# Windowed attention feeding a gated MLP on one core: loads and a shift issued at other steps, block 1's two products mixed, three small copies moved

## The chip, the cores and the metric

The kernel runs on one core of a Trainium2 chip. The metric is the device time of one execution in microseconds. The kernel before took 322.61 us as the median of 3 runs, which lay between 320.56 and 323.91 us.

A core has a tensor engine (PE in the profile, with its weight loads as PEld), a vector engine (DVE), a scalar engine (ACT) and GpSimd (POOL). Each runs its own list of instructions in order and waits on semaphores for the others. SP is a queue that issues transfers and computes nothing. GpSimd issues transfers too, as instructions in its list: while one is being issued, or is waiting, what stands behind it on GpSimd waits as well. The same holds on SP.

## The reference, cut to what matters

```python
# q, k, v: (8 batches, 8 heads, 576 positions, 64 dims), float32
scores = q @ k.T / 8, masked to 0 <= pos_q - pos_k < 64
attn   = softmax(scores)
x      = attn @ v                     # then (4608 tokens, 512 = heads x dims)
h      = x @ w_in                     # (4608, 2048)
g      = h * clip(h + 3, 0, 6) / 6
out    = g @ w_out                    # (4608, 512)
```

Each query sees only the 64 latest keys, so attention is cheap and the two products with w_in and w_out make most of the work.

## The kernel before, in words

**Attention.** A batch has 8 heads, worked on as 4 pairs. The code counts pairs t = 0 to 31, with b = t // 4 the batch and g = t % 4 the pair in it. Pairs 0 to 3 have code of their own (`t_k`, `t_q`, `s_early`, `pv_early`, `x_early`). Every later pair goes through the same steps. `turn` (line 274) transposes its keys and queries on the tensor engine, `turned` (281) copies them out, keys on DVE and queries on ACT. `s_first` and `s_rest` (294, 308) make the scores. `weights` (314 to 333) takes exponentials on ACT and multiplies them by 0/1 band masks, from pair 8 on GpSimd: one product P (326), then one product Pz for each of the two heads (329). `pv` (402) multiplies the masked weights by the values, `pv_out` (411 to 426) divides by the row sums on DVE, and `x_` (440) puts the result, transposed by a transfer of SP's, into xT, the MLP's input. Pairs 4 to 7 use `x_turned` (455 to 461) instead, a transpose on the tensor engine and a copy on ACT.

**Values.** `load_v` (138) brings a batch's values into a tile Un in two large transfers (parts 0 and 1), and 32 rows of a second tile Us in a small one (part 2). `shift` (158, 159) fills the rest of Us with two SP transfers from Un, moved by 32 rows. `pv` needs both: from its third matmul on it reads Us. Tiles alternate between even and odd batches. For batch 0 the shifted tile is made by seven DVE or GpSimd copies instead (`shift_early`, 151 and 153).

**MLP.** Tokens go in 9 blocks of 512. The first product of a block has 16 units, one for each 128 columns of w_in (line 485, 4 matmuls each), each followed by one activation on ACT (497) and one product on DVE (498) into gT. The second product has 4 groups of 128 tokens, each of 4 units (521, 4 matmuls of gT with w_out), and after the last unit a copy on ACT (527) and a transfer out on SP (529). Units stand in a queue `moe`. `weave(n)` emits the next n. `queue_block(kb)` appends a block: it starts with two units left over from the block before, spreads the others that are left over between the 16 first units, and then adds half of the block's own second units.

**Order.** From pair 7 on the loop is `group(t, n)`: `pv(t)`, `turn(t+2)`, scores and weights of pair t+1, `pv_out(t)`, `x_(t)`, and n units of the MLP. Group 7 takes 4 units and groups 8 to 11 also take 4 each: the 12 first units of block 1 that are left, then its 8 queued second units. From group 12 on a group takes 6 units. Behind a group's own instructions come the loads for the next batch. For batch 3 these are: parts 0 and 1 of the values behind group 7; keys and queries of pair 0 and then part 2 of the values behind group 8; keys and queries of pairs 1 to 3 behind groups 9 to 11; and the shift behind group 9. For batches 4 to 7: keys and queries whole behind the first group of the batch before, values behind its second group, the shift behind its third.

**Pairs 4 to 7 and batch 2.** While these pairs go through the loop at line 810, GpSimd issues batch 2's loads. One-element copies into `seen` (lines 778, 808, 835) make GpSimd wait until a given tile is ready, and so hold the loads back. The shift of batch 2 (line 825) stands behind the four outputs of block 0 on SP.

Of the kernel before, what the change touches and what calls it, by code (L numbers as in the profile page):

```python
# [31 lines left out]
VO = 8  # L32
# [4 lines left out]
def kernel(  # L37
# [9 lines left out]
    nc = tc.nc  # L47
    B, H, S, _ = q.shape
    DM, FF = moe_w_in.shape
    NT = B * S  # L50
    NG = H // 2
    SP = S // R
    NW = S // W
    NM = (S + P - 1) // P
    NFC = FF // P
# [27 lines left out]
    xT = consts.tile([P, NG, XR], BF16, name="xT")  # L83
# [31 lines left out]
    def load_qk(b, n=NG, first=0):  # L115
        t = staged[b] if first else stage.tile([P, H, RL * D], BF16, name="qk9", tag="qk")
        hs = slice(2 * first, 2 * (first + n))
        for z, src in enumerate((k, q)):
            nc.gpsimd.dma_start(
                out=t[halves[z], hs], in_=src[b, hs].rearrange("h (p r) d -> p h (r d)", r=RL)  # L120
            )
        return t
# [8 lines left out]
    def load_v(b, whole=False, part=slice(None)):  # L131
        loads = (
            (0, Un[b % 2][:, 0], 2 * P), (2 * P, Un[b % 2][:, 1], 2 * P),
            *(((W, Us[b % 2][:, 0], 2 * P), (W + 2 * P, Us[b % 2][:, 1], 2 * P)) if whole
              else ((4 * P, Us[b % 2][3 * P // 4 : P, 1], W),)),
        )
        for m, to, n in loads[part]:
            nc.gpsimd.dma_start(  # L138
                out=to[:, :, VO : VO + P],
                in_=v[b, :, m : m + n, :].rearrange("h (p r) d -> p h (r d)", r=2),  # L140
            )

    def pads(b, memset):
        for t in (Un[b % 2], Us[b % 2]):
            memset(t[:, :, :, 0:VO], 1.0)
            memset(t[:, :, :, VO + P : VW], 1.0)
# [8 lines left out]
    def shift(b):  # L155

        un, us = Un[b % 2], Us[b % 2]
        nc.sync.dma_start(out=us[0 : P - 32], in_=un[32:P])
        nc.sync.dma_start(out=us[P - 32 : P, 0], in_=un[0:32, 1])
# [60 lines left out]
    def t_q(t):  # L220
        b, g = divmod(t, NG)
        tp = transposed_heads(ps_h, staged[b][0], g)
        nc.scalar.copy(
            out=QT[t][:].rearrange("q (p r) -> q p r", r=R), in_=tp[:].rearrange("q r p -> q p r"),
        )
        for h in range(2):
            nc.vector.tensor_copy(out=QZ[t][halves[h], h], in_=QT[t][halves[h], S - W : S])

    def t_k(t):
        b, g = divmod(t, NG)  # L230
        tp = transposed_heads(ps_acc, staged[b][1], g)
        nc.vector.tensor_copy(
            out=KT[t % 4][:, W:].rearrange("q (p r) -> q p r", r=R),
            in_=tp[:].rearrange("q r p -> q p r"),
        )

    def s_early(t):

        kt, qt = KT[t], QT[t]
        sc = [ps_t.tile([P, NM - 1, 2, W], F32, name="sc", tag="bk") for _ in range(2)]  # L240
        sl = ps_t.tile([P, 2, W], F32, name="sl", tag="bk")

        def off(to, n):
            nc.tensor.matmul(
                to, lhsT=ident[:], rhs=outside[:].unsqueeze(1).to_broadcast([P, n, W]), start=True, stop=False
            )

        for h in range(2):
            off(sc[h][:].rearrange("p m a w -> p (m a) w"), NW - 1)
        for w in range(NW - 1):  # L250
            for h in range(2):
                nc.tensor.matmul(
                    sc[h][:, w // 2, w % 2], lhsT=kt[halves[h], w * W : w * W + P],
                    rhs=qt[halves[h], w * W : (w + 1) * W], start=False, stop=w == NW - 2,
                )
        off(sl[:], 2)
        nc.tensor.matmul(sl[:], lhsT=kt[:, S - W : S + W], rhs=QZ[t][:], start=False, stop=True)
        for h in range(2):
            nc.scalar.activation(
                out=Pz[t][:, h].rearrange("p m a w -> p (m a w)"),  # L260
                in_=sc[h][:].rearrange("p m a w -> p (m a w)"), func=EXP, scale=scale,
            )
        nc.scalar.activation(out=Pl[t][:, :, 0:W], in_=sl[:], func=EXP, scale=scale)
# [187 lines left out]
    def x_turned(t):  # L451
        b, g = divmod(t, NG)
        opg, opg0 = opgs.pop(t)
        tp = ps_t.tile([P, S], BF16, name="xp", tag="bk")
        nc.tensor.transpose(out=tp[:, 0:W], in_=opg0[:].rearrange("p h d -> p (h d)"), identity=ident[0:D, 0:D])
        for m in range(NM - 1):
            nc.tensor.transpose(
                out=tp[:, W + m * P : W + (m + 1) * P],
                in_=opg[:, m // 2, m % 2].rearrange("p h d -> p (h d)"), identity=ident[:],
            )  # L460
        nc.scalar.copy(out=xT[:, g, b * S : b * S + S], in_=tp[:])
# [72 lines left out]
    moe = deque()  # L534

    left = []

    def queue_block(kb, kept=2 * NG):

        f = first_units(kb)  # L540
        moe.extend(left[:2])
        del left[:2]
        n = len(left)
        for i, unit in enumerate(f):
            moe.extend(left[i * n // NFC : (i + 1) * n // NFC])
            moe.append(unit)
        left[:] = second_units(kb)
        n = len(left) - kept
        moe.extend(left[:n])
        del left[:n]  # L550
# [10 lines left out]
    def complete(kb, fcs, pair=()):  # L561
        unit, hidden = units[kb]
        for fc in fcs:
            unit(fc, (NG - 1,), act=fc not in pair)
            if fc in pair[1:]:
                for x in pair:
                    hidden(x)
        for _ in fcs:
            moe.popleft()

    def weave(n):
        for _ in range(min(n, len(moe))):
            moe.popleft()()
# [131 lines left out]
    warm(ps_h, 4, W)  # L705
    t_k(0)
    t_q(0)
    t_k(1)
    t_q(1)
    s_early(0)  # L710
    t_k(2)
    t_q(2)
    s_early(1)
    t_k(3)
    t_q(3)
    s_early(2)
    for m in range(1, NM):
        shift_early(m, nc.vector.tensor_copy)
    s_early(3)
    warm(ps_acc, 4)  # L720
# [23 lines left out]
    def group(t, n):  # L744

        if t >= 2 * NG:
            pv(t)
        if t + 2 < T:
            turn(t + 2)
        if t + 1 < T:  # L750
            host = t + 2
            if host >= T:
                hosts[host] = [ps_h.tile([P, 8 * P], BF16, name=name, tag="bk") for name in ("tk", "tq")]
            s = s_first(t + 1, host)
            weights(t + 1, s, s_rest(t + 1))
        if t >= 2 * NG:
            pv_out(t)
        if t + 2 < T:
            turned(t + 2, 0)
        if t >= 2 * NG:  # L760
            x_(t)
        weave(2)
        if t + 2 < T:
            turned(t + 2, 1)
        weave(n - 2)
# [10 lines left out]
    def behind(t):  # L776

        nc.gpsimd.tensor_copy(out=seen[:], in_=opgs[t][1][0:1, 0, 0:1])
# [16 lines left out]
    for t in range(n, n + 4):  # L795
        if t < n + 3:
            turn(t + 1)
        s = s_first(t, min(t + 1, n + 3))

        def copies():  # L800
            if t < n + 3:
                turned(t + 1, 0)
                turned(t + 1, 1)

        weights(t, s, s_rest(t), own, copies)
        if t < n + 3:
            weave((4, 2, 2)[t - n])
    nc.gpsimd.tensor_copy(out=seen[:], in_=P0[(n + 3) % 4][0:1, 0, 0, 0:1])
    staged[2] = load_qk(2, 1)
    for t in range(n, n + 4):  # L810
        pv(t, t % 2 == 0)
        pv_out(t)
        behind(t)
        if t < n + 2:
            load_v(2, part=(slice(0, 1), slice(1, 3))[t - n])
        else:
            load_qk(2, 1, t - n - 1)
        if t > n:
            x_turned(t - 1)
        if t < n + 3:  # L820
            weave(1)
    turn_two(2 * NG)
    weave(len(moe))
    late[0] = 1
    shift(2)
    queue_block(1)
    u, some = units[1][0], range(NG - 1)
    u(0, some, ps_t)
# [2 lines left out]
    x_turned(n + 3)  # L831
    u(3, some, to=pair_bank()[0])
    complete(1, range(4))
    pads(3, nc.gpsimd.memset)
    nc.gpsimd.tensor_copy(out=seen[:], in_=xT[0:1, NG - 1, S : S + 1])
    load_qk(2, 1, 3)
    group(2 * NG - 1, 4)
    load_v(3, part=slice(0, 2))
    for t in range(2 * NG, T):
        b, g = divmod(t, NG)  # L840
        if g == 0 and b > 2:
            queue_block(b - 1)
        group(t, -(-len(moe) // (NG - g)))
        if t == 2 * NG:
            staged[3] = load_qk(3, 1)
            load_v(3, part=slice(2, 3))
        elif b == 2:
            load_qk(3, 1, g)
        if g == 0 and 3 <= b < B - 1:
            staged[b + 1] = load_qk(b + 1)  # L850
        if g == 1 and 3 <= b < B - 1:
            load_v(b + 1)
        if g == 1 + (b > 2) and b + 1 < B:
            shift(b + 1)
    late[0] = 2
    queue_last(NTB - 2)
    flag = flagged()
# [35 lines left out]
```

## Time and profile before

| | before |
|---|---|
| median of 3 runs | 322.61 us (320.56 to 323.91) |
| the profiled execution | 321.83 us |
| its span, first to last instruction | 320.0 us |
| granted TensorE clock, mean | 0.996 |
| PE busy | 302.5 us (95%) |
| DVE busy | 181.1 us (57%) |
| ACT busy | 184.3 us (58%) |
| POOL busy | 124.1 us (39%) |

A row of the timeline gives the start, the duration, the engine, the line of the kernel, the operation, what it writes and reads, how many instructions are merged in it, and in brackets how long its engine was idle before it and what ended that. A row of the waits gives who waited for whom, the total, the number of times and the longest. A row of the transfers gives the queue, the number, the size of each, and the median time from issue to landing. "issue" as a releaser means that the profile shows nothing that the engine waited for.

### The profile page before, as it was taken

How to read it: one execution, taken by the hardware profiler on the slowest of the kernel's cores; microseconds unless marked ns; L12 is line 12 of the kernel's file. 1: busy time of each engine (PE TensorE's matmuls, PEld its weight loads, DVE VectorE, ACT ScalarE, POOL GpSimd, SP SyncE). 2: the span in 40 equal slices, each digit the busy share in tenths (PEclk: the TensorE clock that was granted, in tenths of full speed). 3: DMA queues.
4: the chain of work that ended last, by engine and by line, in shares of the span. 5: the costliest groups of instructions: out<-in, count | busy, mean ns of one | idle time of the engine just before them, and what ended most of it. 6: DMA issues, size and time to landing. Idle time of an engine off the chain costs nothing.

```text
span 320.0 us, 10694 instructions
## 1 busy us (share of the span) xinstructions
PE 302.5 (95%) x4566; PEld 152.2 (48%) x4608; DVE 181.1 (57%) x415; ACT 184.3 (58%) x345; POOL 124.1 (39%) x169
## 2 busy tenths in 40 slices
PE   7889998889999999999999999999999999999992
PEld 3454454444545555555555555555544444444440
DVE  5776747588747753775377627762776156334200
ACT  2737665578657764776477547764773366454310
POOL 8971204669785435553446335633330000000000
PEclk9999999999999999999999999999999999999998
DMA  7999995989999932994299339934021200100021
GB/s 93 164 203 207 207 189 116 173 146 111 179 124 167 131 116 88 167 128 117 88 155 140 108 98 154 144 102 103 5 63 43 84 33 0 69 33 34 36 74 66
DMA packets 57592, 35.67 MB, mean 111 GB/s; under 512 B 39872, under 2 KB 51648, under 8 KB 57536
## 3 DMA queue, kind: packets, MB, share of 16 engines
q0 software_dynamic: 35904, 18.81, 45.9%
q1 hardware_dynamic: 21632, 16.08, 20.6%
q8 instruction: 38, 0.62, 0.8%
q14 instruction: 18, 0.15, 0.1%
HBM read 37.62 MB, written 9.44 MB: 147 GB/s over the span
## 4 chain that ended last, share of the span: by engine, by line
PE 86%; DMA 5%; DVE 2%; issue 2%; ACT 2%; POOL 1%; SPq 0%; POOLq 0%; ACTq 0%
PE hT L485 37%; PE acc L521 35%; PE o L402 3%; PE s L308 3%; PE acco L521 2%; DMA V<-V 2%; PE tk L274 2%; DMA qk<-in_k_dram 2%; DMA xT<-opl 1%; POOL qk L108 1%; PE tq L274 1%; PE hTo L485 1%; DVE opl L426 0%; DVE V L151 0%; PE xp L373 0%
## 5 line engine op out<-in xcount | busy, mean ns | idle before, releaser
L498 DVE SCALAR_TENSOR_TENSOR gT<-t,hT 128x512 bf16<-128x512 bf16 x141 | 95.7, 686 | 77.7 <-ACT t L497 76.9
L485 PE MATMUL hT<-xT,win 128*128 128x512 bf16 x552 | 132.1, 379 | 0.9 <-ACT xT L376 0.3
L521 PE MATMUL acc<-wout,gT 128*128 128x512 bf16 x518 | 126.1, 379 | 2.4 <-issue 1.3
L497 ACT ACTIVATE t<-hT,half_const 128x512 bf16<-128x512 f32 x141 | 95.7, 689 | 50.0 <-PE hT L485 48.1
L485 PEld LDWEIGHTS <-win 128*128 128x128 bf16 x576 | 55.6, 98 | 66.2 <-issue 1.0
L521 PEld LDWEIGHTS <-gT 128*128 128x128 bf16 x576 | 54.3, 98 | 62.8
L329 POOL TENSOR_TENSOR Pz<-e,band 128x512 bf16<-128x512 bf16 x48 | 54.2, 1146 | 0.5 <-ACT e L321 0.4
L326 POOL TENSOR_TENSOR P<-e,first 64x256 bf16<-64x256 bf16 x24 | 15.9, 661 | 84.7 <-ACT e L317 84.6
L527 ACT COPY osb<-acc 128x512 f32<-128x512 f32 x34 | 19.9, 586 | 43.7 <-PE acc L521 43.7
L321 ACT ACTIVATE e<-s 128x512 bf16<-128x512 f32 x56 | 30.2, 593 | 0.9 <-PE s L308 0.7
L281 DVE COPY KT<-tk 128x576 bf16<-128x576 bf16 x28 | 21.0, 749 | 5.3 <-ACT e L317 4.5
L138 POOL DMA_DIRECT2D V<-in_v_dram x22 | 17.9, 819 | 11.6 <-DMA win<-in_moe_w_in_dram 5.2
L426 DVE TENSOR_TENSOR opl<-o,recs 128x256 bf16<-128x256 f32 x52 | 19.6, 419 | 0.5
L281 ACT COPY QT<-tq 128x576 bf16<-128x576 bf16 x28 | 17.8, 637 | 1.5 <-PE tq L274 1.5
L411 DVE TENSOR_REDUCE sums<-o 128x10 f32<-128x20 f32 x26 | 4.5, 175 | 24.3 <-PE o L402 24.3
L402 PEld LDWEIGHTS <-Pz 64*64 64x64 bf16 x1008 | 11.6, 108 | 13.3 <-issue 11.5
L308 PE MATMUL s<-QT,KT 64*64 64x64 bf16 x896 | 14.7, 195 | 0.5 <-issue 0.5
L317 ACT ACTIVATE e<-tk 64x128 bf16<-64x128 f32 x28 | 7.6, 270 | 12.5 <-PE tq L294 12.5
L402 PE MATMUL o<-V,Pz 64*64 64x65 bf16 x936 | 13.6, 195 | 1.2 <-DMA V<-V 1.2
L274 PE MATMUL tk<-ident,qk 64*64 64x64 bf16 x504 | 13.9, 195 | 0.3 <-DMA qk<-in_k_dram 0.3
L274 PE MATMUL tq<-ident,qk 64*64 64x64 bf16 x504 | 13.7, 195 | 0.4 <-DMA qk<-in_q_dram 0.4
L274 PEld LDWEIGHTS <-qk 64*64 64x64 bf16 x1008 | 11.5, 106 | 3.1 <-issue 1.7
(102 smaller groups left out, 196.6 us busy)
## 6 DMA issues: line engine op xcount, KB each, us to landing
out_dram<-osb SPq DMA_DIRECT2D x36, 256.0 KB, 2.3
V<-in_v_dram POOLq DMA_DIRECT2D x16, 256.0 KB, 5.7
V<-V SPq DMA_DIRECT2D x6, 432.0 KB, 4.3
qk<-in_k_dram POOLq DMA_DIRECT2D x4, 576.0 KB, 6.7
qk<-in_q_dram POOLq DMA_DIRECT2D x4, 576.0 KB, 9.7
wout<-in_moe_w_out_dram POOLq DMA_DIRECT2D x2, 1024.0 KB, 18.8
qk<-in_q_dram POOLq DMA_DIRECT2D x12, 144.0 KB, 4.3
qk<-in_k_dram POOLq DMA_DIRECT2D x12, 144.0 KB, 3.8
```

Of the source, the lines that this page charges most:

```text
L274: nc.tensor.transpose(out=hosts[t][z][halves[h], r * W : (r + 1) * W], in_=staged[b][halves[z], 2 * g + h, r * D : (r + 1) * D], identity= ...
L281: (nc.scalar.copy if z else nc.vector.tensor_copy)(out=(QT[t % 4][:] if z else KT[t % 4][:, W:]).rearrange("q (p r) -> q p r", r=RL), in_= ...
L308: nc.tensor.matmul(ss[h][halves[i], c, m, r], lhsT=keys(t, h, W * (w - 1), r), rhs=QT[t % 4][halves[h], w * W : (w + 1) * W], start=True, ...
L321: nc.scalar.activation(out=e[:].rearrange("p c m r w -> p (c m r w)"), in_=ss[h][:].rearrange("p c m r w -> p (c m r w)"), func=EXP, scale ...
L329: muls[h].tensor_tensor(out=Pw[t % 4][:, h].rearrange("p c m r w -> p (c m) (r w)"), in0=e[:].rearrange("p c m r w -> p (c m) (r w)"), in1 ...
L402: nc.tensor.matmul(o[i][halves[c], c0 : c0 + D + 1], lhsT=p, rhs=vt[:, hh, v0 : v0 + D + 1], start=(r == 0), stop=(r == 1), skip_group_che ...
L426: nc.vector.tensor_tensor(out=opg[:, :, i], in0=ov[i][:, 0:4, 1 : D + 1].rearrange("p (m h) d -> p m h d", h=2), in1=rec[:, i, 0:4].rearra ...
L485: nc.tensor.matmul(hT, lhsT=win16[:, g, fc * P : (fc + 1) * P], rhs=xT[:, g, t0 : t0 + TB], start=(g == 0), stop=(g == NG - 1),)
L497: nc.scalar.activation(out=t1[:], in_=hT, func=RELU, bias=half_const[:], scale=1.0 / 6.0)
L498: nc.vector.scalar_tensor_tensor(out=gT[:, fc, :], in0=t1[:], scalar=1.0, in1=hT, op0=MIN, op1=MULT)
L521: nc.tensor.matmul(acc, lhsT=gT[:, fc, ts * P : (ts + 1) * P], rhs=wout16[:, fc, :], start=(fc == 0), stop=(fc == NFC - 1),)
L527: nc.scalar.copy(out=osb[:], in_=acc)
```

## The change

Five things change.

1. The query copies QZ of pair 3 (line 227) move on DVE from ahead of the shifted values to between the copies for m = 2 and m = 3.
2. Batch 2: part 0 of the values is issued ahead of the keys and queries of pair 0, behind a new one-element copy from batch 1's last value tile. Parts 1 and 2 follow behind pair 4, keys and queries of pairs 1 and 2 behind pairs 5 and 6 (before: 6 and 7), those of pair 3 behind group 7 (before: ahead of it). The shift is issued at pair 6, ahead of the last output of block 0. Two one-element copies go.
3. Block 1's queued units are put in a new order: f stands for a first unit, z for a second one. Groups 7 to 11 emit f f f z | f f f z | f f f f | f f z z | z z z z in place of twelve f and eight z.
4. Batch 3: pair 0 and part 0 of the values behind group 8, pair 1 and then parts 1 and 2 behind group 9, pairs 2 and 3 behind groups 10 and 11, the shift behind group 10. Block 2 is queued with four leftover units in front, where it had two.
5. Batches 4 to 7: keys and queries come pair by pair behind the four groups of the batch before, in place of one load of the whole. Values and shift stay at their groups.

```diff
@@ -223,6 +223,8 @@
         nc.scalar.copy(
             out=QT[t][:].rearrange("q (p r) -> q p r", r=R), in_=tp[:].rearrange("q r p -> q p r"),
         )
+
+    def padded(t):
         for h in range(2):
             nc.vector.tensor_copy(out=QZ[t][halves[h], h], in_=QT[t][halves[h], S - W : S])
 
@@ -535,11 +537,11 @@
 
     left = []
 
-    def queue_block(kb, kept=2 * NG):
+    def queue_block(kb, kept=2 * NG, lead=2):
 
         f = first_units(kb)
-        moe.extend(left[:2])
-        del left[:2]
+        moe.extend(left[:lead])
+        del left[:lead]
         n = len(left)
         for i, unit in enumerate(f):
             moe.extend(left[i * n // NFC : (i + 1) * n // NFC])
@@ -705,16 +707,22 @@
     warm(ps_h, 4, W)
     t_k(0)
     t_q(0)
+    padded(0)
     t_k(1)
     t_q(1)
+    padded(1)
     s_early(0)
     t_k(2)
     t_q(2)
+    padded(2)
     s_early(1)
     t_k(3)
     t_q(3)
     s_early(2)
-    for m in range(1, NM):
+    for m in (1, 2):
+        shift_early(m, nc.vector.tensor_copy)
+    padded(3)
+    for m in range(3, NM):
         shift_early(m, nc.vector.tensor_copy)
     s_early(3)
     warm(ps_acc, 4)
@@ -805,24 +813,28 @@
         weights(t, s, s_rest(t), own, copies)
         if t < n + 3:
             weave((4, 2, 2)[t - n])
+    nc.gpsimd.tensor_copy(out=seen[:], in_=Us[1][0:1, 1, 0, VO : VO + 1])
+    load_v(2, part=slice(0, 1))
     nc.gpsimd.tensor_copy(out=seen[:], in_=P0[(n + 3) % 4][0:1, 0, 0, 0:1])
     staged[2] = load_qk(2, 1)
     for t in range(n, n + 4):
         pv(t, t % 2 == 0)
         pv_out(t)
-        behind(t)
-        if t < n + 2:
-            load_v(2, part=(slice(0, 1), slice(1, 3))[t - n])
-        else:
-            load_qk(2, 1, t - n - 1)
+        if t < n + 3:
+            behind(t)
+        if t == n:
+            load_v(2, part=slice(1, 3))
+        elif t < n + 3:
+            load_qk(2, 1, t - n)
         if t > n:
             x_turned(t - 1)
+        if t == n + 2:
+            shift(2)
         if t < n + 3:
             weave(1)
     turn_two(2 * NG)
     weave(len(moe))
     late[0] = 1
-    shift(2)
     queue_block(1)
     u, some = units[1][0], range(NG - 1)
     u(0, some, ps_t)
@@ -831,27 +843,28 @@
     x_turned(n + 3)
     u(3, some, to=pair_bank()[0])
     complete(1, range(4))
+    f, z = [moe.popleft() for _ in range(NFC - 4)], list(moe)
+    moe.clear()
+    moe.extend(f[0:3] + z[0:1] + f[3:6] + z[1:2] + f[6:] + [z[2], z[4], z[3]] + z[5:])
     pads(3, nc.gpsimd.memset)
-    nc.gpsimd.tensor_copy(out=seen[:], in_=xT[0:1, NG - 1, S : S + 1])
+    group(2 * NG - 1, 4)
     load_qk(2, 1, 3)
-    group(2 * NG - 1, 4)
-    load_v(3, part=slice(0, 2))
     for t in range(2 * NG, T):
         b, g = divmod(t, NG)
         if g == 0 and b > 2:
-            queue_block(b - 1)
+            queue_block(b - 1, lead=4 if b == 3 else 2)
         group(t, -(-len(moe) // (NG - g)))
-        if t == 2 * NG:
-            staged[3] = load_qk(3, 1)
-            load_v(3, part=slice(2, 3))
-        elif b == 2:
-            load_qk(3, 1, g)
-        if g == 0 and 3 <= b < B - 1:
-            staged[b + 1] = load_qk(b + 1)
-        if g == 1 and 3 <= b < B - 1:
-            load_v(b + 1)
-        if g == 1 + (b > 2) and b + 1 < B:
-            shift(b + 1)
+        if b + 1 < B:
+            if g == 0:
+                staged[b + 1] = load_qk(b + 1, 1)
+            else:
+                load_qk(b + 1, 1, g)
+            if b == 2 and g < 2:
+                load_v(b + 1, part=(slice(0, 1), slice(1, 3))[g])
+            if b > 2 and g == 1:
+                load_v(b + 1)
+            if g == 2:
+                shift(b + 1)
     late[0] = 2
     queue_last(NTB - 2)
     flag = flagged()
```

## The prediction

> **What bounds the kernel now.** I read the page's busy times first, then the tensor engine's waits, then a table by stretches, and last the timeline of each queue around the waits.
>
> ```profile
> PE 302.5 (95%) x4566; PEld 152.2 (48%) x4608; DVE 181.1 (57%) x415; ACT 184.3 (58%) x345; POOL 124.1 (39%) x169
> ```
> ```profile
> PE o L402 <- DMA V<-V: 1.2, 1, 1.2
> POOL seen L808 <- DVE P L326: 14.2, 1, 14.2
> PE o L352 <- DVE V L151: 0.2, 1, 0.2
> ```
> ```profile
> 56.00:72.00 16.00, 13.65 (x310) 7.25 (x313) 10.55 (x26) 10.68 (x22) 10.21 (x21) 1.00 1.11 160
> 72.00:92.00 20.00, 19.08 (x509) 10.65 (x512) 14.29 (x38) 14.20 (x31) 16.96 (x22) 1.00 0.96 138
> 92.00:256.00 164.00, 162.42 (x2660) 81.97 (x2679) 98.27 (x217) 101.56 (x193) 68.97 (x76) 1.00 0.64 111
> ```
>
> The tensor engine (PE, the first figure behind the length of each stretch) is the bound. From 92 to 256 us it idles 1.58 us of 164, so nothing moved there can win much. From 56 to 92 us it idles 3.27 us of 36, and GpSimd is at its fullest (16.96 of 20 us in the second stretch). The change is decided there, and a stall that it adds there is paid in full, since PE never catches up.
>
> **The sum, part by part.** Times are on the clock of the trace of before; "moved" means less what PE has won by then.
>
> *Batch 2's loads and shift.*
>
> ```profile
> 63.30 0.21 PE L274 MATMUL tk<-ident,qk 64*64 64x64 bf16 x1 [0.29 <-DMA qk<-in_k_dram]
> 63.96 0.21 PE L274 MATMUL tq<-ident,qk 64*64 64x64 bf16 x1 [0.44 <-DMA qk<-in_q_dram]
> 69.85 0.42 PE L402 MATMUL o<-V,Pz 64*64 64x65 bf16 x29 [1.22 <-DMA V<-V]
> ```
> ```profile
> 53.60 0.91 POOL L138 DMA_DIRECT2D V<-in_v_dram  x1 [0.87 <-issue]
> 54.65 1.45 POOL L138 DMA_DIRECT2D V<-in_v_dram  x2
> 57.00 0.60 POOL L119 DMA_DIRECT2D qk<-in_k_dram  x1 [0.28 <-issue]
> ```
> ```profile
> 62.86 0.64 SPq L158 DMA_DIRECT2D V<-V  x1
> 63.55 0.59 SPq L159 DMA_DIRECT2D V<-V  x1
> 80.94 0.54 SPq L158 DMA_DIRECT2D V<-V  x1
> 81.54 0.59 SPq L159 DMA_DIRECT2D V<-V  x1
> 83.06 1.46 SPq L440 DMA_TRANSPOSE xT<-opl  x1
> 84.57 1.23 SPq L440 DMA_TRANSPOSE xT<-opg  x1
> ```
>
> Three PE waits come from these loads: 0.29 + 0.44 for pair 1's keys and queries, 1.22 for the shift. Part 0 of the values now leaves while GpSimd waits for pair 7's weights (the wait of 14.2 us at line 808), some 3 us ahead of 53.60. Parts 1 and 2 leave in its place, about 1 us ahead of 54.65, and pair 1 follows at once, about 2 us ahead of 57.00. The waits were 0.73 and 1.22, so both should go: -0.73 (between -0.3 and -0.73, as pair 1 now shares the transfer engines with the shift) and -1.22 (between 0 and -1.22). The new one-element copy waits for batch 1's last value tile. It costs nothing inside the 14.2 us of idle time; if that tile came later than pair 7's weights it would hold batch 2's first keys back. The shift waits on SP ahead of block 0's last output, which nobody awaits soon. Pair 3's load moves behind group 7's multiplications and is first read two groups on. I cost that at nothing; if it came late, PE would wait about as it does now for pair 1 (up to +0.7).
>
> *Block 1's units mixed.* First units need ACT and DVE, second ones only PE.
>
> ```profile
> 70.54 0.45 PE L308 MATMUL s<-QT,KT 64*64 64x64 bf16 x30
> 75.27 0.39 PE L308 MATMUL s<-QT,KT 64*64 64x64 bf16 x4
> 75.92 0.41 PE L308 MATMUL s<-QT,KT 64*64 64x64 bf16 x27 [0.26 <-issue]
> ```
>
> Scores that take about 0.45 us in group 8 take 75.27 to 76.33, about 1.06, in group 9, behind four first units whose PSUM tiles DVE had not freed. With a second unit last in group 8 that goes: -0.5 (between 0 and -0.6). Accumulators held in PSUM over a group could give some of it back.
>
> *Pair 3's query copies.*
>
> ```profile
> 14.14 0.68 DVE L227 COPY QZ<-QT 64x64 bf16<-64x64 bf16 x2 [0.46 <-ACT QT L223]
> 17.21 0.30 DVE L151 COPY V<-V 64x576 bf16<-64x576 bf16 x1
> ```
>
> DVE idled 0.46 us before these two copies, and PE waited 0.2 for the last shifted copy. The first shifted copies now fill that idle time, but pair 3's scores take QZ later. I take -0.2 (between +0.2 and -0.4).
>
> So far PE is 0.73 + 1.22 + 0.5 + 0.2 = 2.65 us ahead.
>
> *Batch 3's loads and shift.* Here the change takes time back.
>
> ```profile
> 71.90 2.26 POOL L329 TENSOR_TENSOR Pz<-e,band 128x512 bf16<-128x512 bf16 x2
> 74.11 0.65 POOL L119 DMA_DIRECT2D qk<-in_k_dram  x1
> 74.74 0.61 POOL L119 DMA_DIRECT2D qk<-in_q_dram  x1
> 75.34 0.60 POOL L138 DMA_DIRECT2D V<-in_v_dram  x1
> 76.09 0.66 POOL L326 TENSOR_TENSOR P<-e,first 64x256 bf16<-64x256 bf16 x1
> 77.10 2.26 POOL L329 TENSOR_TENSOR Pz<-e,band 128x512 bf16<-128x512 bf16 x2 [0.35 <-ACT e L321]
> 81.45 0.66 POOL L326 TENSOR_TENSOR P<-e,first 64x256 bf16<-64x256 bf16 x1 [0.90 <-ACT e L317]
> ```
> ```profile
> 84.71 0.45 PE L402 MATMUL o<-V,Pz 64*64 64x65 bf16 x32
> 89.51 0.45 PE L402 MATMUL o<-V,Pz 64*64 64x65 bf16 x32
> ```
> ```profile
> V<-in_v_dram POOLq DMA_DIRECT2D x1, 256.0 KB, 4.5
> ```
> ```profile
> V<-in_v_dram POOLq DMA_DIRECT2D x1, 256.0 KB, 8.1
> ```
> ```profile
> V<-V SPq DMA_DIRECT2D x1, 72.0 KB, 5.0
> ```
> ```profile
> V<-V SPq DMA_DIRECT2D x1, 72.0 KB, 6.3
> ```
>
> (Single transfers, in narrow windows: values issued at 102.50, values at 54.65, the second shift transfers of 81.54 and of 63.55.)
>
> GpSimd first. Group 8's multiplications end at 71.90 + 2.26 - 0.73 - 1.22 - 0.2 = 72.0. Pair 0 (0.65 + 0.61) and part 0 (0.91) follow to 74.2, then group 9's multiplications (0.66 + 2.26) to 77.1, then pair 1 (1.25) to 78.35. Only now comes part 1 (0.91), with part 2 (0.60) to 79.85. Group 10's multiplications would have started at 81.45 - 2.65 = 78.8, so they slip by 1.05 and end at 79.85 + 2.91 = 82.76. Pair 11's products (84.71, moved 82.06) take the second head's weights almost at once. Their slack was 84.71 - (81.45 + 0.66 + 2.25) = 0.35: stall 0.6 (between 0 and 0.8).
>
> Then the shift. Part 1 issued at 78.35 lands 4.5 later at 82.85. On SP the shift now stands behind pair 10's two transposes (83.06 to 85.80, moved to 83.15). It is issued at 83.2 and lands 0.6 + 5.0 later, at 88.8. Pair 12's products, the first to read batch 3's shifted values, are due at 89.51 - 2.65 + 0.6 = 87.46. Before, the shift landed at 81.54 + 5.0 = 86.5, with 3 us to spare. After, PE waits 1.35 us: I take the nearest rows, the same tile's own shift and a value load with a quiet queue. The low end is 0, the high end both slow rows: 78.35 + 8.1 + 0.6 + 6.3 = 93.35, a wait of 5.9. Queued behind that wait are everything on PE, and on SP pair 11's transposes, which block 2 reads only after four leftover units; those four units are what covers them.
>
> *Batches 4 to 7.*
>
> ```profile
> 102.50 2.40 POOL L138 DMA_DIRECT2D V<-in_v_dram  x3
> 107.77 0.66 POOL L326 TENSOR_TENSOR P<-e,first 64x256 bf16<-64x256 bf16 x1 [2.88 <-ACT e L317]
> ```
>
> Three more pairs of issues a batch, 1.25 us each, fall into idle time of GpSimd's, 2.88 us ahead of the next multiplication in this row. The values leave 1.25 us later, and their shift was issued only some 10 us after them. I cost this at nothing; without that idle time it would be 1.25 us for a group that loads.
>
> *The sum.* -2.65 + 0.6 + 1.35 = -0.70 us. The profiled execution took 321.83 us (span 320.0), 0.78 below the median of 322.61. From the one it gives 321.1, from the other 321.9: I take 321.5.
>
> **The rivals.** All start from 322.2, the middle of the two.
>
> - *Batch 3's shift is in time.* For it: its slack was 3 us, and a landing 1.35 us sooner is enough. Against: it now stands behind SP's transposes whatever the load does. Without both stalls: 322.2 - 2.65 = 319.6, and 319.1 if mixing and query copies give their most (0.1 and 0.2 more) and PSUM waits elsewhere go as well.
> - *Slower: batch 3's shift lands late.* One mechanism, one place: the load of part 1 or the shift takes what batch 2's took (8.1 and 6.3). The stall is 5.9 in place of 1.35: 321.5 + 4.55 = 326.0. It turns slower than before from a stall of 2.05 us, and slower by over 1% from about 5.7. Against: those rows stand where the transfer engines were fullest.
> - *The clock.* If PE idles at pair 12 for long, its clock may drop and the next group run slow. The longest wait now is 1.22 us and the granted clock stays 1.00 in its stretch, so no row here shows this. Group 12 lasts 8.6 us, from 89.51 to pair 13's products:
>
> ```profile
> 98.14 0.45 PE o L402 x40
> ```
>
>   A quarter of it at half speed adds 2.1 us, on top of a stall that is longer than forecast: 325 or more. [...]
> - *Batch 2 gains nothing.* Its transfers still land late, now on top of each other: the 1.22 stays, 322.7. For it: one value load took 8.1 us here. Against: some 4 us of lead.
>
> **How the numbers follow.** Forecast 0.60, shift in time 0.22, late shift 0.08, clock 0.02, batch 2 unmoved 0.08. The likeliest gives 321.5. 1% is 3.2 us, about what a measurement of this kernel can tell from no change, so the bounds are 319.4 and 325.8. Faster by over 1% takes 0.13 (somewhat over half of the shift in time), slower by over 1% 0.10 (late shift and clock), and 0.77 stays within. The range is 319.0 to 324.5: below lies the best of the first rival, above the late shift and the clock. The forecast's own range is 320.2 to 323.5.
>
> **What would show it.** The waits of PE for keys and queries near 63 and for V<-V at pair 8 should be gone; a wait for V<-V of 0.5 to 3 us should stand at pair 12, near 87; a short wait for POOL's Pz at pair 11; pair 10's scores should take about 0.45 us; and from 92 us on PE should idle as little as now. If no V<-V wait stands at pair 12, or if PE waits for keys and queries in groups 9 to 11, I am wrong.

## The result, and the profile after

The changed kernel took 324.93 us (median of 22 runs, 322.59 to 327.00), the kernel before 322.00 us (22 runs beside them, 320.56 to 327.66). The ratio is 1.007, with a 95% interval of 1.0042 to 1.0099: slower by 0.7% in its median, within the 1% that counts as no change, but outside the range on record (319.0 to 324.5) and on the other side of the forecast of 321.5. The profiled execution took 324.27 us (span 322.5) against 321.83 us (span 320.0), 2.44 us more.

First the tensor engine's waits of the changed kernel from 56 to 130 us. Its line numbers are two higher than those of before.

```profile
PE o L404 <- DMA V<-V: 1.8, 1, 1.8
PE hT L487 <- DVE gT L500: 0.8, 3, 0.4
PE s L310 <- DVE gT L500: 0.4, 1, 0.4
```

The waits for pair 1's keys and queries are gone, and the 1.22 us for batch 2's shift are gone. A wait of 1.8 us for a shift has come, and several for DVE's gT. The timeline places them:

```profile
63.82 0.44 PE L310 MATMUL s<-QT,KT 64*64 64x64 bf16 x30 [0.36 <-DVE gT L500]
87.86 0.22 PE L404 MATMUL o<-V,Pz 64*64 64x65 bf16 x2
89.91 0.80 PE L404 MATMUL o<-V,Pz 64*64 64x65 bf16 x30 [1.83 <-DMA V<-V]
109.40 1.02 PE L487 MATMUL hT<-xT,win 128*128 128x512 bf16 x4 [0.40 <-DVE gT L500]
```

The first stands where PE waited 0.29 and 0.44 us for pair 1 before. The second and third are pair 12, where the prediction had its new wait: batch 3's shifted values. The last is in group 14, behind the four leftover units now put in front of block 2.

Then the table by stretches, around the wait (length, PE, PEld, DVE, ACT and POOL busy, granted clock, DMA share, GB/s):

```profile
86.60:90.10 3.50, 1.67 (x10) 0.60 (x8) 0.00 (x0) 0.60 (x2) 2.26 (x3) 1.00 0.93 189
90.10:93.50 3.40, 3.38 (x115) 2.21 (x114) 2.26 (x7) 2.01 (x5) 1.43 (x2) 0.51 0.87 233
93.50:97.00 3.50, 3.50 (x18) 1.59 (x17) 0.00 (x0) 0.63 (x2) 2.66 (x4) 0.99 0.43 69
```

PE idles half of the first stretch, all the next one runs at half the clock (0.51), and then it is full again (0.99). So in this execution the wait is paid for twice.

Last the chain of work that ended last, through that wait (start, duration, what), and SP's timeline beside it:

```profile
77.63 1.17 POOL qk L119 x2
78.80 5.39 DMA V<-in_v_dram
...
84.40 5.47 DMA V<-V
...
89.91 0.19 PE o L404
```
```profile
82.16 1.24 SPq L442 DMA_TRANSPOSE xT<-opg  x1
```

GpSimd's list, in order, puts part 1 of the values at 78.80. It lands 5.39 us later, and only then can SP issue the shift, which takes 5.47 us. SP's last instruction before the shift ended at 83.40, so SP was free by then and waited for the values.

### The profile page after: what moved, and what is told of

Its sections match the earlier page's. It is cut to its first block, busy times and chain, and to the rows that moved or that the text cites. A ratio compares the mean times of both kernels' runs of the same rounds, so it can differ in the third digit from the quotient of the medians.

```text
span 322.5 us, 10757 instructions
## 1 busy us (share of the span) xinstructions
PE 306.2 (95%) x4608; PEld 152.4 (47%) x4608; DVE 180.7 (56%) x415; ACT 184.2 (57%) x345; POOL 138.1 (43%) x192
## 4 chain that ended last, share of the span: by engine, by line
PE 83%; DMA 5%; POOL 5%; ACT 2%; DVE 1%; issue 1%; POOLq 0%; SPq 0%; ACTq 0%
PE hT L487 35%; PE acc L523 35%; DMA V<-in_v_dram 3%; PE o L404 3%; PE acco L523 2%; PE s L310 2%; PE tk L276 2%; DMA V<-V 2%; POOL qk L108 2%; POOL Pz L331 1%; ACT t L499 1%; POOL qk L119 1%; PE tq L276 1%; POOL V L127 1%; PE hTo L487 1%
## 5 line engine op out<-in xcount | busy, mean ns | idle before, releaser
L523 PE MATMUL acc<-wout,gT 128*128 128x512 bf16 x544 | 129.9, 381 | 0.0
L119 POOL DMA_DIRECT2D qk<-in_k_dram x26 | 16.7, 644 | 1.3 <-issue 1.3
L119 POOL DMA_DIRECT2D qk<-in_q_dram x26 | 16.0, 614 | 0.0
```

Source lines behind the costliest of these rows:

```text
L119: nc.gpsimd.dma_start(out=t[halves[z], hs], in_=src[b, hs].rearrange("h (p r) d -> p h (r d)", r=RL))
L523: nc.tensor.matmul(acc, lhsT=gT[:, fc, ts * P : (ts + 1) * P], rhs=wout16[:, fc, :], start=(fc == 0), stop=(fc == NFC - 1),)
```

## The experiments

Each ran beside the kernel before on the same chip, in one of three sets; those of a set share the runs of before (medians 321.61, 321.41 and 321.57 us). My main theory was that batch 3's late load and shift make the loss, by the wait and the clock behind it; the rivals are in the texts on record, which name them by letter where there were two.

**Which edit makes the loss.** The first puts only that edit into the kernel before:

```diff
     group(2 * NG - 1, 4)
-    load_v(3, part=slice(0, 2))
...
             staged[3] = load_qk(3, 1)
-            load_v(3, part=slice(2, 3))
+            load_v(3, part=slice(0, 1))
...
             load_qk(3, 1, g)
+            if g == 1:
+                load_v(3, part=slice(1, 3))
...
-        if g == 1 + (b > 2) and b + 1 < B:
+        if g == 2 and b + 1 < B:
             shift(b + 1)
```

> The kernel before with one thing changed: batch 3's values and shift issued where the change puts them (part 0 behind group 8, parts 1 and 2 behind group 9, shift behind group 10). Theory C: this part alone makes the loss. Part 1 leaves at about 80.6 us, lands at about 86, the shift at about 91.5, so PE waits about 2 us at pair 12, and in most runs the clock drops behind it: 323.5 to 325.5. Rival (PE only waits because the rest of the change brought it there 1.7 us sooner): the wait stays below 0.7 us, and the time within 1 us of the kernel before, 321.6.

Measured: 325.76 us against 321.41, ratio 1.0131 (1.0083 to 1.0179). The rows are those of pair 12, and of the clock around it:

```profile
91.68 0.19 PE L402 MATMUL o<-V,Pz 64*64 64x65 bf16 x1 [2.59 <-DMA V<-V]
92.26 0.42 PE L402 MATMUL o<-V,Pz 64*64 64x65 bf16 x29 [0.39 <-DMA V<-V]
```
```profile
88.00:92.00 4.00, 1.28 (x8) 0.43 (x7) 0.00 (x0) 0.58 (x1) 1.88 (x3) 1.00 1.14 209
92.00:96.00 4.00, 3.74 (x116) 2.06 (x116) 2.26 (x7) 1.93 (x5) 2.18 (x3) 0.69 0.66 140
```

This edit alone gives more than the whole loss, and more than was expected of it (about 2 us of wait, 325.5 at most): a wait of 2.98 us at pair 12, with a dip of the clock behind it.

The counterpart is the changed kernel with batch 3's values and shift put back, and pair 3's load put back ahead of group 7 with them:

```diff
-    group(2 * NG - 1, 4)
     load_qk(2, 1, 3)
+    group(2 * NG - 1, 4)
+    load_v(3, part=slice(0, 2))
...
-            if b == 2 and g < 2:
-                load_v(b + 1, part=(slice(0, 1), slice(1, 3))[g])
+            if t == 2 * NG:
+                load_v(3, part=slice(2, 3))
...
-            if g == 2:
+            if g == 1 + (b > 2):
                 shift(b + 1)
```

> The changed kernel with batch 3's values and shift back at their old places, and with pair 3's keys and queries of batch 2 back ahead of group 7, so that GpSimd issues only the values behind group 7. Theory C (the moves on GpSimd hang together: the values stood well behind group 7 only as long as pair 3's load was not there too): no wait for keys and queries in group 9, none for Pz at pair 9, none for V<-V at pair 12; PE keeps a lead of some 1.5 to 2 us past pair 12 and gives 0.4 back in group 14: 320 to 320.8, where the kernel before has 321.6 in these runs. Theory D (GpSimd is too full behind group 7 either way): a wait for Pz at pair 9 of 0.5 us or more stays, 322 or more.

Measured: 321.19 us against 321.41, ratio 0.9994 (0.9967 to 1.002). The loss is gone, though the time stays above the 320 to 320.8 us that were expected. PE's waits from 70 to 130 us:

```profile
PE hT L487 <- DVE gT L500: 0.4, 1, 0.4
PE s L310 <- issue: 0.3, 1, 0.3
```

No transfer stands among them. All that is left of the change together is level with the kernel before, where my sum had -2.65 us for it. (The 0.40 us in group 14, behind the four leftover units, are in it.)

**Load or place on SP.** The prediction had the shift late for two reasons, its load and its place behind two transposes on SP. This one puts only the shift back behind group 9:

```diff
-            if g == 2:
+            if g == 1 + (b > 2):
                 shift(b + 1)
```

> The changed kernel with only batch 3's shift back behind group 9; its values stay where the change put them. Theory A1 (the late load of part 1 holds the shift, which was issued at 84.40 us in the changed kernel, though SP was free at 83.4): the wait at pair 12 stays at 1.5 to 2 us, since SP now waits for the same load with pair 10's transposes queued behind it; time unchanged within 0.7 us of 324.9. Theory A2 (the shift's place on SP behind pair 10's transposes is what counts, as the prediction put it): the wait falls below 0.5 us and the time by 2 us or more.

Measured: 323.40 us against 321.61, ratio 1.0064 (1.0034 to 1.0094). PE's rows for the wait and for the start of pair 13, and the stretches around the wait:

```profile
90.03 0.65 PE L404 MATMUL o<-V,Pz 64*64 64x65 bf16 x30 [1.78 <-DMA V<-V]
98.44 0.45 PE L404 MATMUL o<-V,Pz 64*64 64x65 bf16 x32
```
```profile
86.80:90.30 3.50, 1.68 (x15) 0.65 (x16) 0.00 (x0) 0.59 (x1) 2.23 (x3) 1.00 0.84 178
90.30:93.70 3.40, 3.24 (x119) 2.18 (x120) 0.89 (x5) 2.05 (x5) 1.80 (x3) 1.00 0.91 122
```

The wait stays (1.78 us): the load sets it, and the place on SP does not. In this profile the clock stayed at 1.00 behind the wait, although PE idled as much as in the changed kernel. That makes a comparison: group 12 took 10.41 us here (88.03 to 98.44), 8.63 without its wait, and 8.56 in the kernel before (89.51 to 98.07). With the dip it took 11.80 in the changed kernel (87.86 to 99.66), 9.97 without its wait. The time lies 1.5 us below the changed kernel's 324.93, more than the 0.7 that was expected; the two ratios' intervals overlap, and the mean clock was 0.991 or lower in 6 of these 12 runs, against 15 of the changed kernel's 22.

**Values back without pair 3's load.** Two kernels bring the values back behind group 7 (parts 0 and 1) and group 8 (part 2), but leave pair 3's keys and queries behind group 7, after them. In the first the shift goes back too:

```diff
     group(2 * NG - 1, 4)
+    load_v(3, part=slice(0, 2))
     load_qk(2, 1, 3)
...
-            if g == 2:
+            if g == 1 + (b > 2):
                 shift(b + 1)
```

> The changed kernel with batch 3's values and shift issued where the kernel before had them (values behind groups 7 and 8, shift behind group 9); the rest of the change stays. Theory A (the loss is the 1.83 us wait at pair 12 and the one window at half clock behind it, some 1.5 us): both go, the granted clock stays 1.00 from 88 to 96 us, and the time is 3 to 4 us below the changed kernel's 324.9, about 321, some 1 us below the kernel before. Theory B (the loss is spread over the split loads of batches 4 to 7, block 2's queue and the mixing): the wait goes but the time stays within 1 us of 324.9.

In the second it stays behind group 10:

```diff
     group(2 * NG - 1, 4)
+    load_v(3, part=slice(0, 2))
     load_qk(2, 1, 3)
```

> The changed kernel with only batch 3's values back at groups 7 and 8; the shift stays behind group 10. Theory A1 (late load): the shift goes out as soon as SP is through with pair 10's transposes, at 83 to 83.5 us in place of 84.40, so the wait at pair 12 falls from 1.83 to about 0.9 us; the stall at pair 11 goes too. The clock may then stay up: if so 322 to 322.5, if not 323.5. Theory A2 (place on SP): the wait stays at 1.3 us or more, 323.5 to 325. Theory B: within 1 us of 324.9.

Measured: 326.73 us, ratio 1.0131 (1.0087 to 1.0175), and 326.85 us, ratio 1.0158 (1.0123 to 1.0193), both against 321.61. The times expected of both failed: against their own runs of before they are slower than the changed kernel. PE's waits of the first, from 70 to 96 us, and GpSimd's timeline:

```profile
PE tk L276 <- DMA qk<-in_k_dram: 1.2, 1, 1.2
PE o L404 <- POOL Pz L331: 0.8, 1, 0.8
PE tq L276 <- DMA qk<-in_q_dram: 0.7, 1, 0.7
```
```profile
69.81 1.83 POOL L138 DMA_DIRECT2D V<-in_v_dram  x2
71.61 0.62 POOL L119 DMA_DIRECT2D qk<-in_k_dram  x1
72.20 0.63 POOL L119 DMA_DIRECT2D qk<-in_q_dram  x1
```

The wait for V<-V is gone here, as meant, but two value issues of 1.83 us now stand ahead of pair 3's keys on GpSimd. These come late, and so do the weights behind them, and the clock falls behind these waits (0.85 from 72 to 80 us, 0.72 from 80 to 88 us). In the second kernel, whose shift still stands behind pair 10's transposes, a wait of 0.8 us for V<-V is left, about what was expected. There SP issued the shift at 89.00, just behind these transposes: the place on SP becomes the limit once the values are early. The moves of batch 3's values and of pair 3's load hang together on one queue. This is why the second kernel of the first part puts both back.

**Parts 1 and 2 one place earlier.** They go ahead of pair 1's keys and queries behind group 9:

```diff
+            if b == 2 and g == 1:
+                load_v(b + 1, part=slice(1, 3))
             if g == 0:
                 staged[b + 1] = load_qk(b + 1, 1)
...
-            if b == 2 and g < 2:
-                load_v(b + 1, part=(slice(0, 1), slice(1, 3))[g])
+            if b == 2 and g == 0:
+                load_v(b + 1, part=slice(0, 1))
```

> The changed kernel with parts 1 and 2 of batch 3's values ahead of the keys and queries of pair 13 behind group 9. Theory C (GpSimd's issue of part 1 sets the end of the wait, one for one): part 1 leaves 1.25 us sooner, the shift lands 1.25 us sooner, and the wait at pair 12 falls from 1.83 to about 0.6 us. The keys then leave 1.5 us later; they landed at 83.11 us and were used at 83.4, so a wait of about 1.2 us for keys should stand in group 11 instead: 322 to 323.5 in all. Rival: the wait at pair 12 stays above 1.2 us, 324 or more.

Measured: 323.76 us against 321.57, ratio 1.005 (1.0022 to 1.0079). PE's waits from 70 to 96 us:

```profile
PE o L404 <- DMA V<-V: 1.1, 2, 1.0
PE tk L276 <- DMA qk<-in_k_dram: 0.8, 1, 0.8
PE tq L276 <- DMA qk<-in_q_dram: 0.6, 1, 0.6
```

The wait for the shift falls from 1.8 to 1.1 us, and 1.4 us of waits for the keys and queries that now come second take its place. But the shift did not land sooner. These are its second transfer, and PE's first products of pair 12:

```profile
85.17 6.41 DMA V<-V
```
```profile
90.08 0.22 PE L404 MATMUL o<-V,Pz 64*64 64x65 bf16 x2
```

It landed at 91.58, where the changed kernel's landed at 89.87; the wait is shorter because PE came to pair 12 at 90.08 in place of 87.86. So the expectation that an earlier issue of part 1 shortens the wait one for one (to 0.6 us) failed. One profile can't say why: with the loads where the change puts them, the shift landed between 89.87 and 91.67 in four profiles (the changed kernel, the one with the shift back, and two that follow: with zeros, and with two units ahead of pair 12).

**What the clock costs.** Eight matmuls of zeros, whose result nobody reads, keep PE busy ahead of pair 12's products:

```diff
     def group(t, n):

+        if t == 3 * NG:
+            warm(ps_acc, 8)
         if t >= 2 * NG:
             pv(t)
```

> The changed kernel with 8 matmuls of zeros (1.73 us, results unused) ahead of pair 12's products. They do no work that the output needs; the wait for the shift is spent on them. Theory A (part of the loss is the clock, which drops for one window because PE idles): the end of the wait does not move, yet the granted clock stays 1.00 behind it; the share of runs with a mean clock under 0.992 falls from 15 of 22 to about 1 in 8, and the median to 322.7 to 323.2. Rival (the lower clock has another cause, such as the start): the share stays above half and the median at 324 to 325.

Measured: 323.30 us against 321.41, ratio 1.0058 (1.0026 to 1.009). The table by stretches at the same place:

```profile
86.60:90.10 3.50, 3.50 (x18) 1.47 (x17) 0.00 (x0) 0.93 (x2) 2.60 (x4) 1.00 1.09 203
90.10:93.50 3.40, 3.13 (x121) 2.02 (x119) 2.26 (x7) 1.93 (x5) 1.34 (x2) 1.00 0.95 246
```

The shift is as late as in the changed kernel, but the clock stays full (1.00 in both stretches). The mean granted clock was 0.991 or lower in 15 of the changed kernel's 22 runs, and in 1 of 12 of these. (Of the 87 runs of the kernel before beside the experiments it was that low in 18. The mean is a rough sign: the profile with only batch 3 late shows the dip at a mean of 0.992.) So the idle time lowers the clock in these runs. Filling it takes the excess over before from 2.93 us to 1.89 us; 322.7 to 323.2 us had been expected.

**Useful work in the wait.** Two, and then four, of block 2's leftover units go ahead of pair 12's products (the second edit has 4 in place of 2, and takes no more than are left):

```diff
     def group(t, n):

+        early = 2 if t == 3 * NG else 0
+        weave(early)
         if t >= 2 * NG:
             pv(t)
...
-        weave(n - 2)
+        weave(n - 2 - early)
```

> The changed kernel with two of block 1's leftover second units (8 matmuls, 1.73 us) emitted ahead of pair 12's products in place of behind its scores. No transfer moves. Theory A: the wait for the shift shrinks from 1.83 to 0 to 0.3 us and the tensor engine never idles long enough for its clock to drop: 3 to 3.5 us below the changed kernel's 324.9, about 321.5. Theory B: the time stays within 1 us of 324.9.

> The changed kernel with four leftover second units (16 matmuls, 3.45 us) ahead of pair 12's products. Two of them left a wait of 1.34 us. Theory C: no wait is left at pair 12, PE gains 1.8 us on the changed kernel's undisturbed 322.7 and its clock stays up in nearly all runs: 320.8 to 321.5, no slower than the kernel before. Rival (what fills the wait is paid elsewhere, since pair 13's scores and GpSimd's products for it start 1.7 us later): 322 or more.

Measured: 322.35 us against 321.61, ratio 1.002 (0.9991 to 1.0049), with a wait of 1.34 us left in its profile (0.3 at most had been expected), where the shift landed later than in the changed kernel; and 321.28 us against 321.41, ratio 0.9983 (0.996 to 1.0006). The profiled execution of the second had a mean granted clock of 0.982, so that its span isn't used; its stretches around pair 12 stand at 1.00:

```profile
84.00:92.00 8.00, 7.89 (x143) 4.01 (x143) 5.53 (x15) 5.45 (x11) 7.59 (x10) 1.00 1.25 174
92.00:100.00 8.00, 8.00 (x145) 4.07 (x144) 3.24 (x9) 4.16 (x9) 3.96 (x6) 1.00 0.87 198
```

With four units as cover the late shift costs nothing: the loss is gone with the loads left where the change puts them.

**Batch 2's loads alone, and the mixed order alone,** each put into the kernel before (the main added lines; in the first, pair 3's load stays ahead of group 7):

```diff
+    nc.gpsimd.tensor_copy(out=seen[:], in_=Us[1][0:1, 1, 0, VO : VO + 1])
+    load_v(2, part=slice(0, 1))
...
+        if t == n:
+            load_v(2, part=slice(1, 3))
+        elif t < n + 3:
+            load_qk(2, 1, t - n)
...
+        if t == n + 2:
+            shift(2)
```

> The kernel before with batch 2's loads and shift alone moved (part 0 of the values first, pairs 1 and 2 one step sooner, the shift at pair 6; pair 3 stays ahead of group 7). My prediction had 1.95 us for this. The changed kernel's trace has pair 8's products 1.55 us sooner, since a wait of 0.36 us for DVE's gT and two smaller ones stand where the wait for keys was. So 1.3 to 1.6 us ahead at pair 9, kept to the end as batch 3's shift had 3 us to spare: 1.2 to 1.5 us below the kernel before. Rival: DVE, ACT and GpSimd behind take it back by pair 12: within 0.5 us of the kernel before.

```diff
+    f, z = [moe.popleft() for _ in range(NFC - 4)], list(moe)
+    moe.clear()
+    moe.extend(f[0:3] + z[0:1] + f[3:6] + z[1:2] + f[6:] + [z[2], z[4], z[3]] + z[5:])
```

> The kernel before with block 1's units alone mixed as in the change. My prediction had 0.5 us for this. Expected: pair 10's products 0.5 to 0.7 us sooner against pair 9's, kept to the end: 0.3 to 0.7 us below the kernel before. Rival: accumulators that stay in PSUM over two groups cost as much as the order wins: no difference of 0.2 us or more.

Measured, both against 321.57 us: 321.53, ratio 0.9987 (0.9957 to 1.0016), and 321.28, ratio 0.9986 (0.9953 to 1.002). Neither gain can be told from zero by the times; of the first 1.2 to 1.5 us had been expected. The traces tell more. These are the first products of pairs 8 and 9: of the kernel with only batch 3 late, which has batch 2's loads as before; of the one with the mixed order alone, which has them as before too; and of the one with batch 2's loads moved.

```profile
68.44 0.23 PE L402 MATMUL o<-V,Pz 64*64 64x65 bf16 x4
73.89 0.23 PE L402 MATMUL o<-V,Pz 64*64 64x65 bf16 x4
```
```profile
68.61 0.23 PE L402 MATMUL o<-V,Pz 64*64 64x65 bf16 x4
73.27 0.23 PE L402 MATMUL o<-V,Pz 64*64 64x65 bf16 x4
```
```profile
68.09 0.23 PE L402 MATMUL o<-V,Pz 64*64 64x65 bf16 x4
73.54 0.23 PE L402 MATMUL o<-V,Pz 64*64 64x65 bf16 x4
```

None of them waits for V<-V at pair 8, the first two with the old loads included. Group 8 takes 5.45 us in the old order, whether the loads moved or not, and 4.66 us in the mixed one. The row of the first kernel where pair 1's keys were late in the profile of before shows what stands there when they are not:

```profile
63.92 0.44 PE L308 MATMUL s<-QT,KT 64*64 64x64 bf16 x30 [0.36 <-DVE gT L498]
```

PE waits for DVE instead, there and in group 8 (0.22 us at 70.01). I take it that the waits for transfers had given DVE time to catch up; no run tests that by itself.

**Two leftover units in place of four.** To see what the 0.40 us of group 14 is worth, the kernel of the first part (both back) gets the old number:

```diff
-            queue_block(b - 1, lead=4 if b == 3 else 2)
+            queue_block(b - 1, lead=2)
```

> The kernel of e5_both_back with two leftover units in front of block 2, as before, in place of four. Theory: PE's wait of 0.40 us for DVE's gT in group 14 comes from four first units in a row that the longer front leaves behind; it goes, and the time falls by 0.4 us, to about 0.6 us below the kernel before. Rival: the wait only moves (block 2's first units now come two units sooner and wait for pair 11's transposes): within 0.2 us of e5_both_back, level with the kernel before.

Measured: 321.65 us against 321.57, ratio 0.9984 (0.9957 to 1.0011). PE's wait from 56 to 130 us that is new, and the stretch that holds it:

```profile
PE hT L487 <- DMA xT<-opg: 1.2, 1, 1.2
```
```profile
92.00:96.00 4.00, 3.11 (x15) 1.45 (x16) 1.37 (x2) 1.46 (x3) 1.75 (x3) 1.00 1.16 168
```

The 0.40 us go and 1.2 us come, for the transposes that block 2 reads. So the expected gain of 0.4 us did not come, and the rival, that the wait only moves, holds. The two extra units were the transposes' cover. The granted clock was 1.00 in this stretch.

## Why the prediction was wrong

The starts of pairs 8 and 12 in the two traces carry the account; 21.13 us lay between them before (68.38 to 89.51). In the changed kernel:

```profile
68.30 0.23 PE L404 MATMUL o<-V,Pz 64*64 64x65 bf16 x4
...
99.66 0.23 PE L404 MATMUL o<-V,Pz 64*64 64x65 bf16 x4
107.83 0.23 PE L404 MATMUL o<-V,Pz 64*64 64x65 bf16 x4
116.39 0.23 PE L404 MATMUL o<-V,Pz 64*64 64x65 bf16 x4
```

(Before, pairs 13, 14 and 15 started at 98.07, 106.20 and 114.31.)

| where | forecast, us | in the traces, us |
|---|---|---|
| gain when pair 12 starts | -2.05 | -1.65 (87.86 less 89.51) |
| wait for the shift at pair 12 | +1.35 | +1.83 |
| rest of group 12 | 0 | +1.41 |
| group 13 | 0 | +0.04 |
| group 14 | 0 | +0.45 (8.56 less 8.11) |
| sum at pair 15 | -0.70 | +2.08 (116.39 less 114.31) |

The third row is group 12's 11.80 us less the wait of 1.83 and the 8.56 of before. Behind pair 15 the traces run in step (199.6 and 199.5 us to PE's end).

**The step that failed most: the clock.** The prediction had a lower clock as a rival at 0.02; the sum has no term for it. After 1.83 us of idle time the granted clock was 0.51 for one stretch of 3.4 us. Group 12's rest was 1.41 us longer than before with that dip, and 0.07 us longer (8.63 less 8.56) in the kernel with the shift back, which had the wait without the dip. So the dip cost about 1.34 us there, more than half of the 2.78 us between the forecast and the traces at pair 15. (The rival's 2.1 us, for a quarter of the group at half speed, was my estimate; this profile shows 0.51 for 3.4 us.) Filling the wait saved 1.04 us between medians (2.93 less 1.89). The two groups of the changed kernel's own runs lie 2.6 us apart (322.77 us the median of the 7 at a mean clock of 0.994 or more, 325.41 of the 15 below); not all of that need be the clock, since the wait may differ from run to run too. The clock isn't the whole of the error: even the 7 runs lie 0.8 us above the kernel before, and the table without the dip comes to about +0.7, where the forecast was -0.70. How much idle time brings the dip stays open: a wait of 1.78 us left the clock at 1.00 in one profile (the shift back), and 1.83 us was followed by 0.51 in another (the changed kernel), though PE was busy for 1.68 and 1.67 us of the 3.50 us ahead.

**The wait itself** was placed rightly and sized too small by 0.48 us: part 1 was issued at 78.80 (forecast 78.35) and took 5.39 us (forecast 4.5); the shift took 5.47 behind its issue at 84.40 (forecast 5.6 behind 83.2). Of the two causes named, the place on SP was not one: with the shift put back the wait was 1.78 us all the same. The late load is the cause. How much of it is the issue on GpSimd and how much the time to land is not separated.

**Batch 2's loads: -0.73 and -1.22 were too much.** The first was worth little: pair 8 starts at 68.30 in place of 68.38, and a wait of 0.36 us for DVE took the place of the 0.29 and 0.44. Such starts differ between executions: with the old loads they are 68.38, 68.44 and 68.61, with the loads moved 68.30 and 68.09, so the gain is somewhere from 0.1 to 0.5 us. The second was worth about 0.7: from pair 8 to pair 12 took 21.13 us before, and in the two kernels with the old order and no such wait:

```profile
68.44:88.88 20.44, 19.59 (x514) 10.72 (x513) 15.24 (x38) 14.63 (x31) 17.72 (x22) 1.00 0.85 121
```
```profile
68.09:88.45 20.36, 19.57 (x513) 10.72 (x512) 15.24 (x38) 14.84 (x31) 17.39 (x22) 1.00 1.00 140
```

(Batch 3 late alone, with batch 2's loads as before; batch 2's loads moved alone.) The first of these rows also says that the wait was not a fixed part of the kernel before. Of three profiled executions with the old loads one shows it, the one that I read, in which a value load took 8.1 us. With the wait absent, moving the loads gains 0.08 us on this stretch.

**The mixed order: -0.5** was about right. The kernel with the mixed order alone, and the changed one:

```profile
68.61:88.43 19.82, 19.33 (x514) 10.53 (x514) 15.29 (x38) 14.22 (x31) 17.55 (x22) 1.00 1.06 133
```
```profile
68.30:87.86 19.56, 19.23 (x513) 10.53 (x512) 15.19 (x38) 14.14 (x31) 18.66 (x24) 1.00 1.01 137
```

That is 0.62 us less than the 20.44 and 0.80 less than the 20.36. The scores of pair 10 that were to get shorter did: 0.58 us (at 73.67) in the changed kernel, 1.06 before. In the times (0.9986, 0.9953 to 1.002) it can't be told from nothing.

**Pair 11's stall (+0.6)**, 0.70 by the prediction's own rows (82.76 less 82.06), came at half that size. No wait for Pz stands in PE's list, but pair 11's products took 0.76 us in place of 0.45, and the weight loads among them waited for Pz:

```profile
82.88 0.76 PE L404 MATMUL o<-V,Pz 64*64 64x65 bf16 x32
```
```profile
83.25 0.27 PEld L404 LDWEIGHTS <-Pz 64*64 64x64 bf16 x24 [0.23 <-POOL Pz L331]
```

The group ahead took longer than in the kernel before (5.11 us, 77.77 to 82.88, against 4.79), which let GpSimd catch up in part. **The query copies (-0.2)** show no gain: PE's wait of 0.2 us for the last shifted copy is gone, and one for the query copies stands in its place. No run tests them alone.

```profile
16.38 0.22 PE L259 MATMUL sl<-QZ,KT 128*128 128x128 bf16 x1 [0.32 <-DVE QZ L229]
```

**Batches 4 to 7** cost nothing that shows (0.1 us behind pair 15), as forecast. **Group 14 (+0.45)** was not in the sum at all: I named the four leftover units as cover for the transposes, which they are, and did not ask what they displace. The kernel with two of them shows both sides.

Open: why one execution's value load took 8.1 us, why the shift's landing differs by up to 1.8 us between profiles, and whether the mixed order gains a few tenths. No kernel here beats the one before: the best medians (321.19, 321.28 and 321.28 us, each against its own 321.41, 321.41 and 321.57) all have intervals that hold 1.

## What to carry to other kernels

A wait for a transfer that one trace shows is not a price: look whether it stands in another execution, and what the engine would wait for next, since the idle time may have been another engine's time to catch up (here a wait of 0.36 us for DVE took its place). A stall that a change adds on the tensor engine can have a second price, the clock behind it (0.51 for 3.4 us here); useful work put in front of the waiting instruction saved both here (four units, not two). Loads that share one in-order queue move together: putting back the values alone, with 1.83 us of their issues ahead of pair 3's keys, made things worse than the change itself (ratios of 1.0131 and 1.0158 against 1.007).

## What the runs showed of the hardware

Idle time of TensorE can be followed by a lower clock: behind a wait of 1.83 us (changed kernel) it was 0.51 for 3.4 us, and behind 2.59 and 0.39 us (only batch 3 late) 0.69 for 4 us, while waits of 1.22 us (kernel before), 1.2 us (two leftover units) and 1.78 us (shift back) left it at 1.00. A load of the same 256 KB, issued by the same line, took 4.5, 5.39 or 8.1 us to land in the rows that this document shows. So a price for a landing taken from one row may be off by more than the 2.65 us that this change was summed to gain.
